# Mixture-of-experts kernel: slots of 512, 384 and 256 rows, with every slot from the ninth on inside branches

## The chip, the core and the metric

The kernel runs on one core of one Trainium2 chip. The metric is the device time of one execution in microseconds (us): the median of several runs. A profiled execution has a trace, which is read here. PE is the matrix engine (PEld its weight loads), DVE the vector engine, ACT the scalar engine, POOL GpSimd, and SP the engine that issues most DMAs. A name with a q behind it (ACTq, PEldq) is the engine's sequencer: it waits, branches, loads registers and issues DMAs.

## The reference

The reference is three layers in a row over 4608 tokens of 512 values.

```python
attn_out = _attn_ref(q, k, v)                  # linear attention, 8 x 8 heads
x = attn_out.transpose(0, 2, 1, 3).reshape(4608, 512)
# mixture of experts: 8 experts, each token goes to one
e_idx = np.argmax(x @ w_gate + modality_bias[modality_id], axis=1)
for e in range(8):
    mask = e_idx == e
    h = np.maximum(x[mask] @ w1[e], 0.0)       # 512 -> 1024
    out[mask] = gate_w[mask, None] * (h @ w2[e])   # 1024 -> 512
# a dense layer on top
h = out @ w_in                                 # 512 -> 2048
return np.maximum(0.01 * h, h) @ w_out         # 2048 -> 512
```

With the inputs used here the tokens are very unevenly spread: three experts get 1019, 2289 and 1300 tokens, the other five get none. The counts are known only on the chip, once the gate has been computed.

## The kernel before

The kernel has four stages one after another: attention with the gate (to 185 us), the experts (to 663 us), the first dense product ("hidden", to about 1045 us) and the second one. Every instruction is written out by hand in the order of each engine's queue (`manual_schedule`); an engine runs its queue strictly in that order.

**Slots.** The expert stage works on slots, groups of at most 512 tokens of one expert. `slot_tables` computes on DVE, from the counts, a small table `ti`: for each of up to 16 slots its expert, its first row in `region` (the list of token numbers) and its first column in `dense` (the output), and behind them the number of big slots and of all slots. Big slots come first. An expert with n tokens gets a big slot for each 512 tokens while more than 256 are left, and a slot of 256 rows for a rest of 1 to 256. Here that makes nine big slots (2 + 4 + 3) and one small slot.

**One slot** (`slot(s)`) is two products. `pass1` makes eight blocks of the inner layer, twelve matmuls each (L572, into PSUM bank `hp`); ACT writes relu of each as `hh` (L574), DVE the remainder `hl` (L575). The `hp` banks are three, so the fourth block has to wait until `hl` of the first has been written. `pass2` makes four blocks of the output, 24 matmuls each (L583, bank `yp`), which ACT copies out and stores to `dense` (L589, L590). One slot is thus 96 + 96 = 192 matmuls. All operands are kept as a high and a low part; `split` (L481, L482) makes the two, ACT the high one and DVE the low one.

During slot s its successor is prepared: POOL gathers the successor's tokens (`xload`, L553), ACT scales them (`xgate`), PE transposes them in the second and third block of `pass2` (`xprep`, 16 transposes, L564), SP loads the successor's weights (`wload`, L523) and ACT and DVE split them (`wsplit`).

**Static and branched slots.** The first nine slots (0 to 8) are written out without branches. In slots 0 to 7 the idle time of DVE and ACT is filled by `conversions`, which turn the 64-bit weights of the dense layers into 32-bit ones in steps; its last stores are `wod<-rh` and `wod<-rl` on SP (L635, L636). During slot 8 the first operands of the hidden stage are fetched (`pre`): SP loads the block `xr` of `dense` (L778) ahead of the slot and one of seven weight tiles `wi` (L771) at each step of it, and ACT and DVE split `xr` into operands `x` (`hidden.prep`) in the middle of the last block of `pass2`. The slots from 9 on stand in nested branches:

```python
with tc.If(ns > s):                 # ns: number of all slots
    with tc.If(nb > s) as big:      # nb: number of big slots
        slot(s)
    ...
    with big.Else():
        slot(s, rows=slice(0, SLOT // 2))
    more(s + 1)
```

Every engine executes these branches by itself, from registers that it loads from `ti` (L702, L703). Behind the branches `hidden.late` loads the rest of the first weights, `sums` and `prep` make further operands, and `hidden.run` computes (L801).

Of the kernel before, what the change touches and what calls it, by code (L numbers as in the profile page):

```python
# [421 lines left out]
CLAMP_HI = float(np.array(0x47EFFFFF, np.int32).view(np.float32))  # L422


def slot_tables(tc, con, ps, cst):


    nc = tc.nc
    V = nc.vector
    tb = con.tile([128, NE], BF16, name="ntb")  # L430
# [5 lines left out]
    d = con.tile([128, 2, 17], F32, name="sd")  # L436
    V.memset(d, 0.0)
    g = con.tile([128, 2, NE, 9], F32, name="sg")
    V.tensor_tensor(out=g[:, 0], in0=bc(n[:, :], 2, 9), in1=bc(cst["k512"], 1, NE), op=ALU.is_gt)
    V.scalar_tensor_tensor(out=g[:, 1], in0=bc(n[:, :], 2, 9), scalar=-256.0, in1=bc(cst["k512"], 1, NE), op0=ALU.add, op1=ALU.is_gt)  # L440
    m = con.tile([128, 2, NE], F32, name="sm")
    V.tensor_reduce(out=m, in_=g, axis=AX.X, op=ALU.add)
    b5 = con.tile([128, NE], F32, name="sb5")
    V.tensor_scalar(out=b5, in0=m[:, 1], scalar1=float(SLOT), scalar2=None, op0=ALU.mult)
    V.tensor_copy(out=d[:, 0, 1:9], in_=m[:, 1])
    V.tensor_tensor(out=d[:, 0, 9:17], in0=m[:, 0], in1=m[:, 1], op=ALU.subtract)
    V.tensor_tensor(out=d[:, 1, 1:9], in0=b5, in1=n, op=ALU.min)
# [5 lines left out]
    V.tensor_scalar(out=n1, in0=ci[:, 0, 16:17], scalar1=-1.0, scalar2=None, op0=ALU.add)
    sv = con.tile([128, NSLOT], F32, name="sv")
    V.tensor_scalar(out=sv, in0=cst["iota"], scalar1=n1[:, 0:1], scalar2=None, op0=ALU.min)
    ge = con.tile([128, NSLOT, 17], F32, name="ge")
    V.tensor_tensor(out=ge, in0=bc(sv[:, :], 2, 17), in1=bc(ci[:, 0], 1, NSLOT), op=ALU.is_ge)
    oh = con.tile([128, NSLOT, 16], F32, name="soh")
    V.tensor_tensor(out=oh, in0=ge[:, :, 0:16], in1=ge[:, :, 1:17], op=ALU.subtract)
    t5 = con.tile([128, 16], F32, name="t5")  # L460
    V.tensor_scalar(out=t5, in0=ci[:, 0, 0:16], scalar1=float(SLOT), scalar2=None, op0=ALU.mult)
    v = con.tile([128, 3, 16], F32, name="sv3")
    V.tensor_copy(out=v[:, 0].rearrange("p (a e) -> p a e", a=2), in_=bc(cst["e"], 1, 2))
    V.tensor_tensor(out=v[:, 1, 0:8], in0=cst["eoff"], in1=t5[:, 0:8], op=ALU.subtract)
    V.tensor_tensor(out=v[:, 1, 8:16], in0=cst["eoff"], in1=t5[:, 8:16], op=ALU.subtract)
    V.tensor_tensor(out=v[:, 1, 8:16], in0=v[:, 1, 8:16], in1=b5, op=ALU.add)
    V.tensor_tensor(out=v[:, 2], in0=ci[:, 1, 0:16], in1=t5, op=ALU.subtract)
# [17 lines left out]
def experts(ctx, tc, cst, a, region, xd, dense, did, wops, pre):  # L485
    nc = tc.nc
# [20 lines left out]
    cnt = [0, 0]  # L507
    stage, regs = {}, {}
# [25 lines left out]
    def wsplit(s, which, c):  # L534
# [7 lines left out]
        loads_to(n + 1 + AHEAD)  # L542

    def idload(s):
        if s < NSLOT:
            nc.sync.dma_start(out=idts[s % 3].rearrange("p t c -> p (t c)"),
                              in_=region[bass.ds(reg(s, 1, NE * NT), SLOT), :].rearrange("(p t) c -> p (t c)", t=4))
# [105 lines left out]
                yield  # L653
        store()

    def slot(s, step=lambda: None, mid2=lambda t: None, rows=slice(0, SLOT)):
        if s + 1 < NSLOT:
            xload(s + 1)
        for f in range(8):
            pass1(f, rows)  # L660
            if f % 2 == 0:
                wsplit(s, 2, f // 2)
            else:
                step()
        if s + 1 < NSLOT:
# [36 lines left out]
    nb = nc.values_load(ti[0:1, 3 * NSLOT:3 * NSLOT + 1], min_val=0, max_val=NSLOT)  # L702
    ns = nc.values_load(ti[0:1, 3 * NSLOT + 1:3 * NSLOT + 2], min_val=NSTATIC, max_val=NSLOT)  # L703

    def more(s):
        if s == NSLOT:
            return
        with tc.If(ns > s):  # L708
            before = dict(stage), list(cnt), nload[0]
            regs.clear()  # L710
            with tc.If(nb > s) as big:
                slot(s)
            stage.clear()
            stage.update(before[0])
            cnt[:], nload[0] = before[1:]
            regs.clear()
            with big.Else():
                slot(s, rows=slice(0, SLOT // 2))
            regs.clear()
# [271 lines left out]
def build(ctx: ExitStack, tc, a, out, dbg=None):  # L991
# [13 lines left out]
    with tc.manual_schedule():  # L1005
# [108 lines left out]
```

## Time and profile before

| | |
|---|---|
| median of 3 runs | 1421.89 us (1420.99 to 1422.07) |
| profiled execution | 1421.04 us, span of its trace 1419.2 us |
| PE busy over the span | 92% (weight loads 86%) |
| DVE, ACT, POOL busy | 74%, 41%, 20% |
| mean granted PE clock | 0.972 |
| slot 8 (static, 512 rows) on PE | 589.75 to 636.60 us |
| slot 9 (in a branch, 256 rows) on PE | 637.39 to 662.80 us |
| hidden stage starts on PE | 669.35 us |

The profile's times count from the start of the span; what lies around the span is 1421.04 - 1419.2 = 1.8 us. A busy share says how full an engine is over the whole run; what one stage is worth is read from that stage's own rows.

### The profile page before, as it was taken

To read this page: it belongs to the slowest core of one execution; us is meant where nothing else is said; L and a number is where in the kernel's file an instruction comes from. 1 tells how busy PE (TensorE), PEld (TensorE's weight loads), DVE (VectorE), ACT (ScalarE), POOL (GpSimd) and SP (SyncE) were. 2 spreads that over 40 slices of the span, in tenths; PEclk is the share of its full clock that TensorE was granted. 3 is DMA by queue.
4 is the path that set the end of the run, shared out by engine and by line. 5 is a ranking of instruction groups with operands and counts; after the bars stand their busy time and mean duration, and the time that the engine had idled before them with its cause. 6 is when DMAs were issued, how large, how long until landed. Compare 5 with 4: busy or idle time off the path is not lost.

```text
span 1419.2 us, 23583 instructions
## 1 busy us (share of the span) xinstructions
PE 1311.5 (92%) x9189; PEld 1224.6 (86%) x9189; DVE 1047.6 (74%) x1504; ACT 586.8 (41%) x924; POOL 289.0 (20%) x249
## 2 busy tenths in 40 slices
PE   5987719999999999998999999999989999999998
PEld 5876717778777877787999999999989999999998
DVE  4889846867786777746677777787767777877785
ACT  3545415455545554556223323232333333333342
POOL 0004431101110011001334343434321101111111
PEclk9999869999999999999999999999999999999999
DMA  9763246778777878686933332333595343434330
GB/s 371 284 246 127 76 156 232 259 240 279 259 255 247 275 254 263 194 311 195 407 146 134 135 119 104 136 148 120 233 417 205 122 134 123 149 120 134 119 119 30
DMA packets 146970, 279.57 MB, mean 197 GB/s; under 512 B 18208, under 2 KB 70432, under 8 KB 145952
## 3 DMA queue, kind: packets, MB, share of 16 engines
q1 hardware_dynamic: 122064, 208.46, 43.1%
q10 hardware_dynamic: 17232, 48.48, 8.7%
q0 software_dynamic: 7552, 21.02, 4.1%
q8 instruction: 75, 1.23, 0.4%
q14 instruction: 47, 0.39, 0.1%
HBM read 181.59 MB, written 96.32 MB: 196 GB/s over the span
## 4 chain that ended last, share of the span: by engine, by line
issue 26%; DVE 8%; PE 7%; POOL 6%; DMA 3%; ACT 1%; POOLq 0%; SPq 0%; DVEq 0%
PE hp L801 7%; POOL out L982 3%; DMA wi<-wid 2%; POOL s L841 2%; DVE ht L814 1%; DMA hd<-ht 1%; DVE ht L850 1%; DVE ht L847 1%; DVE s L838 1%; DVE x L482 1%; DVE ht L834 1%; DVE s L836 1%; POOL s L842 1%; DVE xl L482 0%; ACT ht L843 0%
## 5 line engine op out<-in xcount | busy, mean ns | idle before, releaser
L801 PE MATMUL hp<-xh,wi 128*128 128x256 f32 x1152 | 212.8, 281 | 4.2 <-DVE ht L850 2.3
L960 PE MATMUL yp<-wi,x 128*128 128x256 f32 x1152 | 191.2, 283 | 0.6 <-DVE x L482 0.6
L801 PEld LDWEIGHTS hp<-xh,wi 128*128 128x128 f32 x1152 | 179.4, 188 | 6.8 <-DVE ht L850 3.7
L960 PE MATMUL yp<-wi,wi 128*128 128x256 f32 x1200 | 178.2, 283 | 0.3 <-DVE wi L482 0.3
L801 PE MATMUL hp<-x,wi 128*128 128x256 f32 x1296 | 164.5, 286 | 9.2 <-ACTq L708 6.4
L801 PEld LDWEIGHTS hp<-x,wi 128*128 128x128 f32 x1296 | 161.0, 195 | 9.6 <-ACTq L708 6.6
L960 PEld LDWEIGHTS yp<-wi,wi 128*128 128x128 f32 x1200 | 163.5, 192 | 0.5 <-DVE wi L482 0.5
L960 PEld LDWEIGHTS yp<-wi,x 128*128 128x128 f32 x1152 | 161.5, 192 | 0.8 <-DVE x L482 0.8
L801 PE MATMUL hp<-xl,wi 128*128 128x256 f32 x576 | 160.7, 279 | 0.0
L553 POOL DMA_INDIRECT xg<-xd,idi x44 | 55.6, 1264 | 398.6 <-DVE hl L575 331.6
L572 PE MATMUL hp<-xh,w1h 128*128 128x512 f32 (+1 forms) x320 | 122.9, 384 | 11.8 <-DVE hl L575 11.2
L583 PE MATMUL yp<-hh,w2h 128*128 128x512 f32 (+1 forms) x320 | 122.9, 384 | 0.0
L572 PE MATMUL hp<-xl,w1h 128*128 128x512 f32 (+1 forms) x320 | 121.6, 380 | 0.0
L572 PE MATMUL hp<-xh,w1l 128*128 128x512 f32 (+1 forms) x320 | 121.6, 380 | 0.0
L583 PE MATMUL yp<-hl,w2h 128*128 128x512 f32 (+1 forms) x320 | 121.5, 380 | 0.0
L583 PE MATMUL yp<-hh,w2l 128*128 128x512 f32 (+1 forms) x320 | 121.4, 379 | 0.0
L982 POOL DMA_INDIRECT out<-yo,idx x36 | 47.4, 1317 | 315.9 <-DVE idx L976 294.3
L482 DVE TENSOR_TENSOR w1l<-st,w1h 128x1024 fp32r<-128x1024 f32 x44 | 53.8, 1227 | 76.5 <-ACT w1h L481 74.1
L801 PEld LDWEIGHTS hp<-xl,wi 128*128 128x128 f32 x576 | 108.0, 187 | 0.0
L814 DVE SCALAR_TENSOR_TENSOR ht<-ht 128x1024 f32<-128x1024 f32 x72 | 104.9, 1457 | 2.5
L841 POOL TENSOR_TENSOR s<-s,s 128x512 f32<-128x512 f32 x36 | 48.7, 1352 | 209.3 <-DVE s L838 163.8
L843 ACT ACTIVATE ht<-s 128x512 f32<-128x512 f32 x36 | 22.8, 633 | 151.5 <-POOL s L842 147.0
(202 smaller groups left out, 2583.5 us busy)
## 6 DMA issues: line engine op xcount, KB each, us to landing
st<-in_w SPq DMA_DIRECT2D x89, 512.0 KB, 6.5
hd<-ht ACTq DMA_DIRECT2D x72, 512.0 KB, 2.9
xt<-hd SPq DMA_DIRECT2D x18, 1024.0 KB, 5.3
hr<-hd SPq DMA_DIRECT2D x18, 1024.0 KB, 5.2
wi<-wid SPq DMA_DIRECT2D x28, 512.0 KB, 10.3
wi<-wod SPq DMA_DIRECT2D x6, 2048.0 KB, 13.1
v<-in_v SPq DMA_DIRECT2D x16, 650.0 KB, 9.7
k<-in_k SPq DMA_DIRECT2D x16, 576.0 KB, 9.4
```

Source lines behind the costliest of these rows:

```text
L482: nc.vector.tensor_tensor(out=lo, in0=src, in1=hi.bitcast(F32), op=ALU.subtract)
L553: nc.gpsimd.indirect_dma_start(out=xg[:, t], out_offset=None, in_=xd, in_offset=bass.IndirectOffsetOnAxis(ap=idi[:, t:t + 1], axis=0), bou ...
L572: nc.tensor.matmul(hp[:, rows], lhsT=w[:, k, 128 * f:128 * f + 128], rhs=x[:, k, rows], start=(n == 0), stop=(n == 11))
L583: nc.tensor.matmul(yp[:, rows], lhsT=w[:, f, 128 * d:128 * d + 128], rhs=h[:, f, rows], start=(n == 0), stop=(n == 23))
L801: self.nc.tensor.matmul(bank[:, g], lhsT=w[:, h, k, 128 * g:128 * g + 128], rhs=x[:, k], start=(n == 0), stop=(n == 5))
L814: V.scalar_tensor_tensor(out=c, in0=c, scalar=0.01, in1=c, op0=ALU.mult, op1=ALU.max)
L834: V.tensor_tensor(out=h[:, 0, 0], in0=bank, in1=s[1], op=ALU.add)
L836: V.tensor_tensor(out=s[6], in0=bank, in1=s[1], op=ALU.add)
L841: G.tensor_tensor(out=s[6], in0=s[6], in1=s[5], op=ALU.add)
L843: nc.scalar.activation(out=h[:, 1, 1], in_=s[5], func=AF.Relu)
L960: nc.tensor.matmul(bank, lhsT=x[:, k], rhs=w[i][:, h, k], start=(c == 0), stop=(c == 23))
L982: ins = nc.gpsimd.indirect_dma_start(out=out, out_offset=bass.IndirectOffsetOnAxis(ap=idi[s % 2][:, t:t + 1], axis=0), in_=y[:, t], in_off ...
```

## The change

The change has four parts. (1) `slot_tables` knows three sizes: a rest of 385 to 512 tokens gets 512 rows, one of 257 to 384 gets 384 rows, and one of 1 to 256 gets 256 rows. For the inputs here (1300 = 2 x 512 + 276) there are now eight big slots, one of 384 and one of 256 rows. (2) Eight slots (0 to 7) are static and all from slot 8 on stand in branches. (3) The branch on the number of slots has an Else: the last slot runs a body with `ahead=False`, which gathers, transposes, loads and splits nothing for a successor. (4) `pre` is no longer spread over a slot: all its loads and both `prep`s stand in one piece between slot 7 and the branches.

```diff
-NSTATIC = 9
+NSTATIC = 8
+SIZES = (512, 384, 256)
...
-    V.tensor_tensor(out=g[:, 0], in0=bc(n[:, :], 2, 9), in1=bc(cst["k512"], 1, NE), op=ALU.is_gt)
-    V.scalar_tensor_tensor(out=g[:, 1], in0=bc(n[:, :], 2, 9), scalar=-256.0, in1=bc(cst["k512"], 1, NE), op0=ALU.add, op1=ALU.is_gt)
+    for i in range(3):
+        V.scalar_tensor_tensor(out=g[:, i], in0=bc(n[:, :], 2, 9), scalar=float(-(384, 256, 0)[i]), in1=bc(cst["k512"], 1, NE),
+                               op0=ALU.add, op1=ALU.is_gt)
...
-    pr = con.tile([128, NSLOT, 3, 16], F32, name="spr")
+    pr = con.tile([128, NSLOT, 3, NV], F32, name="spr")
...
-    def slot(s, step=lambda: None, mid2=lambda t: None, rows=slice(0, SLOT)):
-        if s + 1 < NSLOT:
+    def slot(s, rows=slice(0, SLOT), step=lambda: None, ahead=True):
+
+        if ahead:
             xload(s + 1)
...
-        for s in range(NSTATIC - 1):
+        for s in range(NSTATIC):
             slot(s, step=lambda: next(conv, None))
         for _ in conv:
             pass
-    load, prep = pre()
-    slot(NSTATIC - 1, step=lambda: next(load, None), mid2=lambda t: prep() if t == 3 else None)
...
+    pre()
+    nb, nm, ns = (nc.values_load(...) for i in range(3))
...
+    def sized(s, ahead):
+        k = kept()
...
+        with tc.If(nb > s) as big:
+            one(0)
+        with big.Else():
+            with tc.If(nm > s) as middle:
+                one(1)
+            with middle.Else():
+                one(2)
 
     def more(s):
-        if s == NSLOT:
+        if s + 1 == NSLOT:
+            sized(s, False)
             return
...
+        k = kept()
+        with tc.If(ns > s + 1) as again:
+            sized(s, True)
             more(s + 1)
+        with again.Else():
+            restore(k)
+            sized(s, False)
...
-                    def loads():
-                        for i in ORDER:
-                            hidden.wload(0, i)
-                            yield
-
-                    return loads(), lambda: (hidden.prep(0, 1), hidden.prep(0, 2))
+                    for i in ORDER:
+                        hidden.wload(0, i)
+                    hidden.prep(0, 1)
+                    hidden.prep(0, 2)
```

Where the change moves instructions is seen in the built order of each engine. First ACT's queue before the change, from the end of slot 7 into slot 8 and, behind the dots, into slot 8's last block (`xr` is the block of `dense`, `x` its split operand, `y` the copy of an output block):

```order
L481 CAST w1h<-st_2171 128x4x256
L481 CAST rh<-r 128x1792
L574 ACTIVATE hh<-hp 128x512
L481 CAST w2h<-st_2172 128x1024
...
L481 CAST x_5256<-xr_5255 128x512 x2
L589 COPY y_2183<-yp 128x512
```

The two casts of `x` stood behind all relus of slot 8. ACT's queue at the same place after the change; the body that follows the branches here is that of 512 rows, and those of 384 and 256 rows begin alike:

```order
L486 CAST w1h<-st_2174 128x4x256
L486 CAST rh<-r 128x1792
L486 CAST x_5259<-xr_5258 128x512 x2
L710 TENSOR_LOAD ti x3
L743 COMPARE_AND_BRANCH
L730 COMPARE_AND_BRANCH
L582 ACTIVATE hh<-hp 128x512
L486 CAST w2h<-st_2175 128x1024
```

The casts now stand ahead of every relu of slot 8, and so do three register loads and the branches. The second place is PE's queue around the branched slots. Before, from the end of the static slot 8, with the body of 512 rows, its jump to the end, and the branch for the next slot behind the body of 256 rows:

```order
L583 MATMUL yp<-hl,w2h 128x512
L702 TENSOR_LOAD ti
L703 TENSOR_LOAD ti
L708 COMPARE_AND_BRANCH
L711 COMPARE_AND_BRANCH
L572 MATMUL hp<-xh,w1h 128x512
...
L711 UNCONDITIONAL_BRANCH
...
L583 MATMUL yp<-hl,w2h 128x256
L711 UNCONDITIONAL_BRANCH
L708 COMPARE_AND_BRANCH
```

After the change, from the end of the static slot 7 over the three bodies of slot 8 to the branch for the next one:

```order
L710 TENSOR_LOAD ti x3
L743 COMPARE_AND_BRANCH
L730 COMPARE_AND_BRANCH
L580 MATMUL hp<-xh,w1h 128x512
...
L730 UNCONDITIONAL_BRANCH
L733 COMPARE_AND_BRANCH
L580 MATMUL hp<-xh,w1h 128x384
...
L733 UNCONDITIONAL_BRANCH
L580 MATMUL hp<-xh,w1h 128x256
...
L743 COMPARE_AND_BRANCH
```

The body of a slot is now picked by two branches in place of one, and a body that is run stands in front of or between others that are jumped over. The third place is the end of PE's branches after the change: the last body of the Else for slot 8, which stands behind all others, and the hidden stage:

```order
L730 UNCONDITIONAL_BRANCH
L733 COMPARE_AND_BRANCH
L580 MATMUL hp<-xh,w1h 128x384
...
L733 UNCONDITIONAL_BRANCH
L580 MATMUL hp<-xh,w1h 128x256
...
L591 MATMUL yp<-hl,w2h 128x256
L733 UNCONDITIONAL_BRANCH
L829 MATMUL hp<-x_5259,wi_5260 128x256 x36
```

The Else bodies stand in the reverse order of the slots, so that slot 9's Else is followed by the three bodies of slot 8's Else, and these by the hidden stage (L829, before L801).

## Rows read from the trace of the kernel before

**Rows 1.** The page: its span, and the queue of PE's instructions (packets, MB).

```profile
span 1419.2 us, 23583 instructions
...
q8 instruction: 75, 1.23, 0.4%
```

**Rows 2.** Stages of slot 8 and 9: stretch, length, busy (instructions) by engine, clock, DMA.

```profile
589.75:636.60 46.85, 45.69 (x209) 37.42 (x207) 24.17 (x29) 24.03 (x31) 5.78 (x4) 1.00 0.80 275
637.39:662.80 25.41, 25.13 (x208) 24.82 (x208) 16.49 (x21) 18.18 (x27) 4.48 (x4) 1.00 0.67 213
```

**Rows 3.** Timeline of PE: start, length, instruction, idle time before and its releaser.

```profile
636.14 0.39 PE L583 MATMUL yp<-hh,w2l 128*128 128x512 f32 x1
636.37 0.39 PE L583 MATMUL yp<-hl,w2h 128*128 128x512 f32 x1
637.39 0.38 PE L572 MATMUL hp<-xh,w1h 128*128 128x256 f32 x1 [0.64 <-ACT y L589]
...
637.85 0.28 PE L572 MATMUL hp<-xh,w1h 128*128 128x256 f32 x1
637.97 0.28 PE L572 MATMUL hp<-xl,w1h 128*128 128x256 f32 x1
...
662.65 0.28 PE L583 MATMUL yp<-hl,w2h 128*128 128x256 f32 x1
669.35 3.33 PE L801 MATMUL hp<-x,wi 128*128 128x256 f32 x14 [6.43 <-ACTq L708]
...
703.85 4.38 PE L801 MATMUL hp<-x,wi 128*128 128x256 f32 x23 [2.78 <-DMA wi<-wid]
```

**Rows 4.** Line 711, the branch over the big body: duration ns, start us.

```profile
L711 PEldq COMPARE_BRANCH  x1: 3352/3352/3352, 634.0 to 634.0; - x1
...
L711 ACTq COMPARE_BRANCH  x1: 50/50/50, 638.8 to 638.8; - x1
```

**Rows 5.** Line 708 from 660 to 670 us, the branch out: shortest/median/longest ns, starts.

```profile
L708 PEldq COMPARE_BRANCH  x2: 192/2640/5088, 660.6 to 665.9; - x2
...
L708 ACTq COMPARE_BRANCH  x2: 37/41/45, 663.8 to 669.5; - x2
```

**Rows 6.** Line 702, the register loads ahead of the branches.

```profile
L702 PEldq TENSOR_LOAD <-ti x1: 777/777/777, 632.5 to 632.5; - x1
```

**Rows 7.** DMA queues from 634.0 to 637.5 us, the stretch of PE's first branch.

```profile
q8 instruction: 1, 0.02, 1.7%
```

**Rows 8.** Timeline of SP: start, length, DMA issued.

```profile
599.27 0.45 SPq L778 DMA_DIRECT2D xr<-dense  x1
...
670.26 0.82 SPq L771 DMA_DIRECT2D wi<-wid  x2
```

**Rows 9.** DMA issues from 598 to 600 us: size, us from issue to landing.

```profile
xr<-dense SPq DMA_DIRECT2D x1, 1024.0 KB, 7.8
```

**Rows 10.** Timeline of ACT around the start and the end of slot 8.

```profile
594.75 1.69 ACT L481 CAST rh<-r 128x1792 fp32r<-128x1792 f32 x1 [2.76 <-DVE r L631]
...
633.30 1.14 ACT L481 CAST x<-xr 128x512 fp32r<-128x512 f32 x2
```

**Rows 11.** Timeline of DVE at the start of slot 8.

```profile
598.49 0.69 DVE L575 SCALAR_TENSOR_TENSOR hl<-hp,hh 128x512 fp32r<-128x512 f32 x1
```

**Rows 12.** Waits during slot 8: us in total, times, longest.

```profile
PE hp L572 <- DVE hl L575: 1.2, 1, 1.2
```

**Rows 13.** Stretches behind the branches: length, busy by engine, clock, DMA share, GB/s.

```profile
666.00:670.00 4.00, 0.65 (x3) 0.68 (x4) 0.48 (x2) 0.00 (x0) 0.00 (x0) 0.51 0.21 72
670.00:673.00 3.00, 3.00 (x16) 3.00 (x16) 2.97 (x6) 1.87 (x4) 0.00 (x0) 0.52 0.60 160
...
676.00:700.00 24.00, 24.00 (x205) 24.00 (x204) 16.56 (x20) 5.24 (x9) 8.81 (x7) 1.00 1.03 405
```

**Rows 14.** Timeline of DVE at the end of the table.

```profile
190.53 0.95 DVE L471 TENSOR_REDUCE sr<-spr 128x48 f32<-128x768 f32 x1
```

**Rows 15.** Timeline of SP behind the table.

```profile
194.00 0.36 SPq L546 DMA_DIRECT2D idt<-region  x1
```

More of the change, by code (lines that the diff above doesn't have):

```diff
@@ L442, in slot_tables @@
+    for i in range(3):
+        V.scalar_tensor_tensor(out=g[:, i], in0=bc(n[:, :], 2, 9), scalar=float(-(384, 256, 0)[i]), in1=bc(cst["k512"], 1, NE),
+                               op0=ALU.add, op1=ALU.is_gt)
+    m = con.tile([128, 3, NE], F32, name="sm")
     V.tensor_reduce(out=m, in_=g, axis=AX.X, op=ALU.add)
     b5 = con.tile([128, NE], F32, name="sb5")
-    V.tensor_scalar(out=b5, in0=m[:, 1], scalar1=float(SLOT), scalar2=None, op0=ALU.mult)
-    V.tensor_copy(out=d[:, 0, 1:9], in_=m[:, 1])
@@ L446, in slot_tables @@
-    V.tensor_tensor(out=d[:, 0, 9:17], in0=m[:, 0], in1=m[:, 1], op=ALU.subtract)
+    V.tensor_scalar(out=b5, in0=m[:, 0], scalar1=float(SLOT), scalar2=None, op0=ALU.mult)
+    V.tensor_copy(out=d[:, 0, 1:9], in_=m[:, 0])
+    V.tensor_tensor(out=d[:, 0, 9:25].rearrange("p (a e) -> p a e", a=2), in0=m[:, 1:3], in1=m[:, 0:2], op=ALU.subtract)
     V.tensor_tensor(out=d[:, 1, 1:9], in0=b5, in1=n, op=ALU.min)
-    V.tensor_tensor(out=d[:, 1, 9:17], in0=n, in1=d[:, 1, 1:9], op=ALU.subtract)
-    ci = con.tile([128, 2, 17], F32, name="ci")
+    V.tensor_tensor(out=n, in0=n, in1=d[:, 1, 1:9], op=ALU.subtract)
@@ L450, in slot_tables @@
+    V.tensor_tensor(out=d[:, 1, 9:25].rearrange("p (a e) -> p a e", a=2), in0=d[:, 0, 9:25].rearrange("p (a e) -> p a e", a=2),
+                    in1=bc(n[:, :], 1, 2), op=ALU.mult)
+    ci = con.tile([128, 2, NV + 1], F32, name="ci")
     for f in range(2):
-        V.tensor_tensor_scan(out=ci[:, f], data0=cst["one"][:, 0:17], data1=d[:, f], initial=0.0, op0=ALU.mult, op1=ALU.add)
+        V.tensor_tensor_scan(out=ci[:, f], data0=cst["one"][:, 0:NV + 1], data1=d[:, f], initial=0.0, op0=ALU.mult, op1=ALU.add)
@@ L452, in slot_tables @@
     n1 = con.tile([128, 1], F32, name="n1")
[L453 removed]
+    V.tensor_scalar(out=n1, in0=ci[:, 0, NV:NV + 1], scalar1=-1.0, scalar2=None, op0=ALU.add)
     sv = con.tile([128, NSLOT], F32, name="sv")
     V.tensor_scalar(out=sv, in0=cst["iota"], scalar1=n1[:, 0:1], scalar2=None, op0=ALU.min)
[L456 to L457 removed]
@@ L458, in slot_tables @@
[L458 to L463, printed above, removed]
+    ge = con.tile([128, NSLOT, NV + 1], F32, name="ge")
+    V.tensor_tensor(out=ge, in0=bc(sv[:, :], 2, NV + 1), in1=bc(ci[:, 0], 1, NSLOT), op=ALU.is_ge)
@@ L464, in slot_tables @@
+    oh = con.tile([128, NSLOT, NV], F32, name="soh")
+    V.tensor_tensor(out=oh, in0=ge[:, :, 0:NV], in1=ge[:, :, 1:NV + 1], op=ALU.subtract)
+    t5 = con.tile([128, NV], F32, name="t5")
+    V.tensor_scalar(out=t5, in0=ci[:, 0, 0:NV], scalar1=float(SLOT), scalar2=None, op0=ALU.mult)
+    v = con.tile([128, 3, NV], F32, name="sv3")
+    V.tensor_copy(out=v[:, 0].rearrange("p (a e) -> p a e", a=3), in_=bc(cst["e"], 1, 3))
+    V.tensor_tensor(out=b5, in0=b5, in1=cst["eoff"], op=ALU.add)
     V.tensor_tensor(out=v[:, 1, 0:8], in0=cst["eoff"], in1=t5[:, 0:8], op=ALU.subtract)
-    V.tensor_tensor(out=v[:, 1, 8:16], in0=cst["eoff"], in1=t5[:, 8:16], op=ALU.subtract)
@@ L466, in slot_tables @@
-    V.tensor_tensor(out=v[:, 1, 8:16], in0=v[:, 1, 8:16], in1=b5, op=ALU.add)
-    V.tensor_tensor(out=v[:, 2], in0=ci[:, 1, 0:16], in1=t5, op=ALU.subtract)
-    pr = con.tile([128, NSLOT, 3, 16], F32, name="spr")
+    V.tensor_tensor(out=v[:, 1, 8:24].rearrange("p (a e) -> p a e", a=2), in0=bc(b5[:, :], 1, 2),
+                    in1=t5[:, 8:24].rearrange("p (a e) -> p a e", a=2), op=ALU.subtract)
+    V.tensor_tensor(out=v[:, 2], in0=ci[:, 1, 0:NV], in1=t5, op=ALU.subtract)
+    pr = con.tile([128, NSLOT, 3, NV], F32, name="spr")
@@ L473, in slot_tables @@
     V.tensor_tensor(out=r[:, :, 1:3], in0=r[:, :, 1:3], in1=bc(sv[:, :], 2, 2), op=ALU.add)
-    ti = con.tile([128, NSLOT * 3 + 2], I32, name="ti")
     V.tensor_copy(out=ti[:, 0:NSLOT * 3], in_=r.rearrange("p s f -> p (s f)"))
-    V.tensor_copy(out=ti[:, NSLOT * 3:NSLOT * 3 + 2], in_=ci[:, 0, 8:17:8])
-    return ti
+    V.tensor_copy(out=ti[:, NSLOT * 3:NSLOT * 3 + 3], in_=ci[:, 0, 8:25:8])
 def split(nc, hi, lo, src):
@@ L490, in experts @@
     ps2 = ctx.enter_context(tc.tile_pool(name="ps_m2", bufs=2, space=PSUM, reuse_waits="tile"))
-    ti = slot_tables(tc, ctx.enter_context(tc.tile_pool(name="tab", bufs=1, reuse_waits="tile")), ps, cst)
+    ti = wp.tile([128, NSLOT * 3 + 3], I32, name="ti")
+    with tc.tile_pool(name="tab", bufs=1, reuse_waits="tile") as tab:
+        slot_tables(tc, tab, ps, cst, ti)
     w1h = wp.tile([128, 4, F1], F32R, name="w1h")
@@ L532, in loads_to, with wsplit @@
             nload[0] += 1
-    def wsplit(s, which, c):
+    def wsplit(s, which, c, ahead=True):
         n = 8 * s + 4 * (which - 1) + c
@@ L654, in conversions @@
         store()
-    def slot(s, step=lambda: None, mid2=lambda t: None, rows=slice(0, SLOT)):
-        if s + 1 < NSLOT:
+    def slot(s, rows=slice(0, SLOT), step=lambda: None, ahead=True):
+        if ahead:
             xload(s + 1)
@@ L661, in slot @@
             if f % 2 == 0:
-                wsplit(s, 2, f // 2)
+                wsplit(s, 2, f // 2, ahead)
             else:
                 step()
-        if s + 1 < NSLOT:
+        if ahead:
             xgate(s + 1)
@@ L669, in slot @@
                           in_=idts[s % 3].rearrange("p t c -> p (t c)"))
-        idload(s + 2)
+        if ahead:
+            idload(s + 2)
         for t in range(4):
             def mid():
-                if s + 1 < NSLOT and t in (1, 2):
+                if ahead and t in (1, 2):
                     xprep(2 * t - 2)
                     xprep(2 * t - 1)
-                mid2(t)
             pass2(t, o, mid, rows)
-            if s + 1 < NSLOT:
+            if ahead:
                 wsplit(s + 1, 1, t)
@@ L699, in experts, with kept, restore, one @@
             pass
-    load, prep = pre()
-    slot(NSTATIC - 1, step=lambda: next(load, None), mid2=lambda t: prep() if t == 3 else None)
-    nb = nc.values_load(ti[0:1, 3 * NSLOT:3 * NSLOT + 1], min_val=0, max_val=NSLOT)
-    ns = nc.values_load(ti[0:1, 3 * NSLOT + 1:3 * NSLOT + 2], min_val=NSTATIC, max_val=NSLOT)
+    pre()
+    nb, nm, ns = (nc.values_load(ti[0:1, 3 * NSLOT + i:3 * NSLOT + i + 1], min_val=(0, 0, NSTATIC + 1)[i], max_val=NSLOT)
+                  for i in range(3))
+    def kept():
+        return dict(stage), list(cnt), nload[0]
+    def restore(k):
+        regs.clear()
+        stage.clear()
+        stage.update(k[0])
+        cnt[:], nload[0] = k[1:]
+    def sized(s, ahead):
+        k = kept()
+        def one(i):
+            restore(k)
+            slot(s, slice(0, SIZES[i]), ahead=ahead)
+            regs.clear()
+        with tc.If(nb > s) as big:
[5 more added lines that the diff above has]
+                one(2)
     def more(s):
-        if s == NSLOT:
+        if s + 1 == NSLOT:
+            sized(s, False)
             return
[L708 to L719, printed above, removed]
+        k = kept()
+        with tc.If(ns > s + 1) as again:
+            sized(s, True)
             more(s + 1)
+        with again.Else():
+            restore(k)
+            sized(s, False)
     more(NSTATIC)
```

10 lines of the change are left out of this document (5 added, 5 removed).

## The prediction

> **What bounds the kernel now.** I first read the page for its span, 1419.2 us [rows 1], and then the two slots that change as stretches of their own. In slot 8 PE is busy for 45.69 of 46.85 us, in slot 9 for 25.13 of 25.41, both at a granted clock of 1.00 [rows 2]. So a slot is PE's time, and columns are what it pays for. The timeline of PE gives the price of a matmul as the distance of two starts: 0.23 us with 512 columns (636.14 to 636.37) and 0.12 with 256 (637.85 to 637.97) [rows 3]. A slot has 192 of them: with 0.2267 (the stretch of slot 8 less its stall and transposes) 43.5 us at 512 columns and 23.0 at 256. No row has 384 columns; halfway gives 0.173 us, thus 33.3 us a slot, an estimate.
>
> The second thing to read is what PE does between slots, because the change moves work into branches. PE stands idle 0.64 us ahead of slot 9 and 6.43 us ahead of the hidden stage [rows 3]. The rows of the branches say why. The branch on PE's sequencer that skips one body of 512 rows takes 3352 ns from 634.0 us, while the same skip takes 50 ns on ACT [rows 4]. The jump out of everything takes PE 5088 ns from 660.6 us, and ACT comes to its next branch behind it only at 669.5, after 663.8 [rows 5]. In the stretch of the skip the queue of instructions moves one packet [rows 7], 1.23 MB over 75 packets being 16 KB each [rows 1]: so I read the 3.35 us as the wait for the instructions behind the skip. It costs little today because the sequencer runs ahead: it comes to the register loads at 632.5 [rows 6], 4.1 us before slot 8 ends at 636.6 [rows 2], and to the jump out 2.2 us before slot 9 ends at 662.8. That lead is what hides a jump. At 384 columns I take 3.1 us, between the two.
>
> [...]
>
> Behind the branches DMA is the bound, not PE: SP issues the next `wi` at 670.26 us [rows 8], 7.5 us after slot 9's end. From 676 to 700 the DMA engines are full (1.03 at 405 GB/s) [rows 13], and at 703.85 PE still has waited 2.78 us for `wi` [rows 3].
>
> **The change, part by part.**
>
> Slot 8 gets narrower: 43.5 - 33.3 = 10.2 us less. Its 16 transposes stay. The old stall in it, PE's wait of 1.2 us for `hl` [rows 12] (about 1.5 with its edges), goes into the new one: -1.5.
>
> Slot 8 gets an entry: three register loads at 0.78 us [rows 6] where there were none, and one skip over the body of 512 rows at 3.35, in all 5.7 us against a lead of 4.1. PE starts some 1.2 us late: +1.2.
>
> Slot 8 gets a new wait. ACT runs its queue in order, and the two casts of `x` now stand ahead of every relu. They need `xr`. SP issues that load only at 599.27 [rows 8], behind the last stores of the conversion, whose cast ran at 594.75 on ACT [rows 10], and it takes 7.8 us to land [rows 9]: 607.1. Nothing of the change makes its issue earlier; the slot's other loads now come behind the `wi` loads, so it meets a little less traffic, and I take 606. Then two casts in 1.14 us [rows 10], DVE's remainder of the second, a relu, and `hl` at 0.69 [rows 11]: the first bank is free at about 609.0. PE has three banks: 36 matmuls of 0.173 from 591.0 fill them by 597.2. It then stands until 609.0: +11.8 (10 to 13). Queued behind the cast on ACT are all relus and the casts of `w2`, and on DVE all `hl`; PE waits for them. At this place the entry's 1.2 us cost nothing of their own: a later start only shortens the stall.
>
> [...] Slot 8: +1.5. Sum for slot 8: -10.2 - 1.5 + 1.2 + 11.8 + 1.5 = **+2.8**.
>
> Slot 9 gets a chain of jumps, since PE's sequencer must find one body among many: out of the body of 384 rows over that of 256 (the target is near and probably fetched with what came before: 0.1 to 1.5, I take 0.9), then the far jump to the last slot's bodies (5.09; as little as 3.35), then a skip over 512 rows and one over 384 rows, 3.35 each. That is 12.7 us, less the lead of 3.1: a gap of 9.0 to 9.6, I take 9.3, where PE moved on within 0.8 (636.60 to 637.39): +8.5. Starting at the low clock costs +1.5. With no successor there are no transposes and little to stall for: 23.0 in place of 25.4, -2.4. Sum **+7.6**. That a jump is costly by waiting for instructions and not by the branch itself is what the 50 ns on ACT against 3352 on PE show [rows 4]. [...]
>
> The exit gets shorter: the last body runs out with near skips on SP, ACT, DVE and POOL, where they jumped over all 16 slots before. SP can issue `wi` some 0.4 us behind slot 9's end, not 7.46. PE has one far jump, 5.09 less a lead of 2.2, so 2.9 us idle for 6.55, and it no longer waits 2.78 us for `wi`; both and the clock give more than 7, so the DMA bound decides: **-7.0**.
>
> The tables get two more operations on DVE and wider ones: the reduction of 768 values takes 0.95 us [rows 14], with 1152 half as much again, and its product too; two small ones beside: 1.55 us in all. The next consumer, the load of `idt` at 194.00 [rows 15], follows 2.5 us behind the reduction, so some of it may be covered; I take about half: **+0.7** (0 to 1.5).
>
> The sum is 2.8 + 7.6 - 7.0 + 0.7 = **+4.1 us**. From the profiled execution, 1421.04, that makes 1425.1; the median of the runs shown is 0.85 above it, so the median becomes **1426.0**.
>
> **The rivals.**
>
> *Same as before, by cheaper jumps and an early `xr`.* If the far jump costs 3.35 like the near one (-1.7) and `xr` lands at 604 (-2), the sum is +0.4: 1422.3. For it: with two prices in one trace, 3.35 and 5.09, the far one may have been slowed by what else ran at 660 to 666. Against: right behind it, at 666 to 670, DMA moves only 72 GB/s [rows 13].
>
> *Faster: a skip over one body is free.* If PE holds the skipped instructions already, the two skips ahead of slot 9 go (-6.7), and the stop of 2.9 us left costs half as much clock (-0.8): 1426.0 - 7.5 = 1418.5. [...] For it: 3.35 was measured once, behind a whole slot of straight instructions, where the sequencer might have had little time to fetch ahead. Against: the packet in that very stretch.
>
> *Slower still: fetches and loads collide.* SP issues seven `wi` in one piece. If they hold up `xr` or the jumps (every skip at 5.09: +3.5; `xr` 2 us later: +2), the time is 1429.5 to 1431.5. For it: at the skip that I took the price from the DMA queues were nearly empty, while the new jumps come with the `wi` loads behind them. Against: seven tiles of 128 x 1024 values are 3.7 MB, at 405 GB/s [rows 13] about 9 us, long through when slot 9 begins.
>
> **How the numbers follow.** My forecast has a chance of 0.42, with a range of 1425 to 1429; the collision 0.15; the cheaper jumps 0.28; the free skip 0.15. The first two are slower, so 0.57; about 0.2% or 2.8 us is what a measurement can tell from no change, and the third falls within it (0.28), the fourth below (0.15). The range reaches from the free skip, 1418.5, to the collision, 1432; what it leaves out is a sum in which several terms miss in one direction, for example an `xr` that has landed before ACT asks (up to 11 us less).
>
> **What the new profile would show.** Right, if ACT's cast of `x` stands at about 606 with a wait of 8 us or so for the load of `xr`; if PE has one stop of 10 to 13 us within the first 36 matmuls of slot 8, released by `hl`; if PE stands some 9 us ahead of slot 9 with three branches on its sequencer of 5.1, 3.4 and 3.4 us; if the clock is 0.5 behind both stops; if SP issues `wi` within 1 us of slot 9's end. Wrong, if the skips show as 0.1 us, if `xr` is there before 600, or if the wait for `wi` stays and takes back what the exit gives.

## The result and the profile after

The changed kernel takes 1440.36 us (median of 4 runs, 1438.66 to 1441.76) where the kernel before takes 1421.44; the ratio is 1.0134, 95% interval 1.0116 to 1.0151. That is 19 us slower, against a forecast of 4, and outside the range (1418.5 to 1432). The profiled execution took 1438.66 us with a span of 1436.9, 17.6 us more than that of before, and the trace shows where they are.

PE's timeline first: start, length, instruction, idle time before and what ended it.

```profile
596.18 0.43 PE L580 MATMUL hp<-xh,w1h 128*128 128x384 f32 x1 [1.82 <-issue]
...
602.19 0.33 PE L580 MATMUL hp<-xl,w1h 128*128 128x384 f32 x1
602.37 0.34 PE L580 MATMUL hp<-xh,w1l 128*128 128x384 f32 x1
615.34 0.69 PE L580 MATMUL hp<-xh,w1h 128*128 128x384 f32 x1 [12.63 <-DVE hl L583]
615.82 0.52 PE L580 MATMUL hp<-xl,w1h 128*128 128x384 f32 x1
616.14 0.52 PE L580 MATMUL hp<-xh,w1l 128*128 128x384 f32 x1
...
646.13 0.34 PE L591 MATMUL yp<-hl,w2h 128*128 128x384 f32 x1
657.61 0.55 PE L580 MATMUL hp<-xh,w1h 128*128 128x256 f32 x1 [11.14 <-issue]
...
681.96 0.28 PE L591 MATMUL yp<-hl,w2h 128*128 128x256 f32 x1
683.70 4.57 PE L829 MATMUL hp<-x,wi 128*128 128x256 f32 x36 [1.46 <-DMA dense<-y]
...
716.49 4.55 PE L829 MATMUL hp<-x,wi 128*128 128x256 f32 x36 [2.61 <-DMA wi<-wid]
```

A matmul of 384 columns takes 0.17 us, as estimated. PE makes three blocks of slot 8 and stands for 12.63 us; then it runs at 0.32 us a matmul. It stands 11.14 us ahead of slot 9, but only 1.46 ahead of the hidden stage, where it stood 6.43 before [rows 3]. What holds slot 8 is on ACT's timeline:

```profile
599.20 1.70 ACT L486 CAST rh<-r 128x1792 fp32r<-128x1792 f32 x1 [2.76 <-DVE r L639]
611.46 1.14 ACT L486 CAST x<-xr 128x512 fp32r<-128x512 f32 x2 [10.56 <-DMA xr<-dense]
612.84 0.49 ACT L582 ACTIVATE hh<-hp 128x384 fp32r<-128x384 f32 x1 [0.24 <-issue]
```

The first relu of slot 8 comes at 612.84, behind casts that waited 10.56 us for `xr`. The branches on PE's sequencer between slot 8 and slot 9 (shortest/median/longest ns, first and last start), and the granted clock (behind the POOL column) in the 4.3 us after the first stop, during the second one, and in the 3.1 us after it:

```profile
L743 PEldq COMPARE_BRANCH  x2: 92/2611/5130, 591.9 to 643.6; - x2
L733 PEldq COMPARE_BRANCH  x2: 377/2680/4984, 643.2 to 652.5; - x2
L730 PEldq COMPARE_BRANCH  x1: 3562/3562/3562, 648.8 to 648.8; - x1
```

```profile
615.34:619.66 4.32, 4.32 (x13) 4.32 (x14) 3.14 (x4) 0.70 (x2) 3.38 (x3) 0.50 1.03 409
...
646.46:657.61 11.15, 0.01 (x2) 0.04 (x1) 1.22 (x1) 1.52 (x2) 0.00 (x0) 0.68 0.26 75
657.61:660.72 3.11, 3.11 (x14) 3.11 (x15) 0.00 (x0) 0.12 (x1) 0.00 (x0) 0.50 0.02 5
```

All this is where the prediction put it, but for the wait for `wi`, which it took as gone. One thing it did not have at all. The last matmul of the kernel ends at 1425.1 us, 10.7 later than before (1414.3), but the span ends 17.6 later. Behind the last matmul GpSimd drains its queue (the closing line of the kernel, first before and then after the change):

```profile
L1110 POOLq DRAIN  x3: 40/113/3406, 1414.8 to 1419.0; - x3
```

```profile
L1136 POOLq DRAIN  x3: 40/113/10433, 1425.6 to 1436.6; - x3
```

The longest of the three drains takes 10.4 us where it took 3.4. From stage to stage (the start of a matmul plus its spacing as the end of a slot; each row is rounded by itself) the 17.6 us are:

| stage | forecast | measured |
|---|---|---|
| up to the end of slot 7 | +0.7 | +4.5 |
| slot 8 with its entry | +2.8 | +5.3 |
| stop ahead of slot 9, and slot 9 | +7.6 | +9.6 |
| from there to the wait for `wi` (703.85, now 716.49) | -7.0 | -6.6 |
| on to the last matmul | 0 | -1.9 |
| behind the last matmul | 0 | +6.9 |

### The profile page after: what moved, and what is told of

It reads as the page before. It is cut to its first block, busy times and chain, and to the rows that moved or that the text cites. A ratio compares the mean times of both kernels' runs of the same rounds, so it can differ in the third digit from the quotient of the medians.

```text
span 1436.9 us, 23488 instructions
## 1 busy us (share of the span) xinstructions
PE 1302.1 (91%) x9173; PEld 1222.7 (85%) x9173; DVE 1039.5 (72%) x1497; ACT 575.3 (40%) x912; POOL 283.4 (20%) x245
## 4 chain that ended last, share of the span: by engine, by line
PE 31%; issue 30%; DVE 16%; POOL 7%; DMA 5%; ACT 3%; SPq 0%; DVEq 0%; POOLq 0%; ACTq 0%
PE yp L591 14%; PE hp L580 9%; PE hp L829 3%; POOL out L1010 3%; POOL s L869 3%; DVE ht L842 2%; DMA hd<-ht 2%; DVE ht L875 1%; DVE s L866 1%; DVE ht L878 1%; PE tp L572 1%; DVE ht L862 1%; PE xp L247 1%; DVE s L864 1%; DVE x L487 1%
## 5 line engine op out<-in xcount | busy, mean ns | idle before, releaser
L829 PE MATMUL hp<-xh,wi 128*128 128x256 f32 x1152 | 212.8, 281 | 4.4 <-DVE ht L878 2.4
L829 PEld LDWEIGHTS hp<-xh,wi 128*128 128x128 f32 x1152 | 179.4, 188 | 7.0 <-DVE ht L878 3.6
L829 PE MATMUL hp<-x,wi 128*128 128x256 f32 x1296 | 161.6, 283 | 4.1 <-DMA wi<-wid 2.6
L829 PEld LDWEIGHTS hp<-x,wi 128*128 128x128 f32 x1296 | 158.1, 191 | 4.4 <-DVE ht L878 2.8
L829 PE MATMUL hp<-xl,wi 128*128 128x256 f32 x576 | 160.7, 279 | 0.0
L580 PE MATMUL hp<-xh,w1h 128*128 128x512 f32 (+2 forms) x320 | 123.5, 386 | 37.1 <-DVE hl L583 24.2
L561 POOL DMA_INDIRECT xg<-xd,idi x40 | 50.6, 1265 | 377.7 <-DVE hl L583 346.1
L580 PE MATMUL hp<-xl,w1h 128*128 128x512 f32 (+2 forms) x320 | 122.0, 381 | 0.0
L580 PE MATMUL hp<-xh,w1l 128*128 128x512 f32 (+2 forms) x320 | 121.6, 380 | 0.0
L591 PE MATMUL yp<-hh,w2h 128*128 128x512 f32 (+2 forms) x320 | 120.9, 378 | 0.0
L591 PE MATMUL yp<-hl,w2h 128*128 128x512 f32 (+2 forms) x320 | 119.6, 374 | 0.0
L591 PE MATMUL yp<-hh,w2l 128*128 128x512 f32 (+2 forms) x320 | 119.5, 373 | 0.0
L829 PEld LDWEIGHTS hp<-xl,wi 128*128 128x128 f32 x576 | 108.0, 187 | 0.0
L580 PEld LDWEIGHTS hp<-xh,w1h 128*128 128x128 f32 x320 | 62.2, 194 | 51.5 <-DVE hl L583 27.9
L487 DVE TENSOR_TENSOR w1l<-st,w1h 128x1024 fp32r<-128x1024 f32 x40 | 48.8, 1224 | 67.1 <-ACT w1h L486 67.0
```

Of the source, the lines that this page charges most:

```text
L487: nc.vector.tensor_tensor(out=lo, in0=src, in1=hi.bitcast(F32), op=ALU.subtract)
L561: nc.gpsimd.indirect_dma_start(out=xg[:, t], out_offset=None, in_=xd, in_offset=bass.IndirectOffsetOnAxis(ap=idi[:, t:t + 1], axis=0), bou ...
L580: nc.tensor.matmul(hp[:, rows], lhsT=w[:, k, 128 * f:128 * f + 128], rhs=x[:, k, rows], start=(n == 0), stop=(n == 11))
L591: nc.tensor.matmul(yp[:, rows], lhsT=w[:, f, 128 * d:128 * d + 128], rhs=h[:, f, rows], start=(n == 0), stop=(n == 23))
L829: self.nc.tensor.matmul(bank[:, g], lhsT=w[:, h, k, 128 * g:128 * g + 128], rhs=x[:, k], start=(n == 0), stop=(n == 5))
```

## The experiments

The theory after the result: the casts ahead of the relus make the stop in slot 8; the skips over bodies make that ahead of slot 9; and the four gathers that the last slot no longer issues (112 gathers and scatters on GpSimd in place of 116) make the long drain. Rivals stand in the expectations. Ratios are to the kernel before, timed on the same chip, with 95% intervals.

**The splits of `xr` moved back.**

```
-    pre()
+    prep = pre()
...
-            slot(s, slice(0, SIZES[i]), ahead=ahead)
+            slot(s, slice(0, SIZES[i]), ahead=ahead, mid2=lambda t: prep() if s == NSTATIC and t == 3 else None)
...
-                    hidden.prep(0, 1)
-                    hidden.prep(0, 2)
+                    return lambda: (hidden.prep(0, 1), hidden.prep(0, 2))
```

> The changed kernel, but the two splits of xr stand in the last block of slot 8 again, inside the bodies, as before the change; its loads stay in one piece ahead of the branches. If the casts of x, which wait for the load of xr ahead of all relus, make PE stand 12.6 us in slot 8, this stop goes, and with it the 1.9 us of low clock behind it: 14.5 us less than the changed kernel, about 1426 us. Rival: the seven wi loads in one piece fill the DMA queues, so that the next thing to wait for in slot 8 (the w2 weights or the tokens of slot 9) is late instead: PE then stands as long at another place, and the time stays within 3 us of the changed kernel's 1440.

Measured: 1433.41 us, ratio 1.0081 (1.0052 to 1.0110), 7 us less than the changed kernel, between the 14.5 expected and the rival's 3. The stop of 12.6 us is gone, and about half of it comes back in other places:

```profile
604.22 0.44 PE L580 MATMUL hp<-xh,w1h 128*128 128x384 f32 x1 [2.02 <-DVE hl L583]
629.28 0.66 PE L572 MATMUL tp<-cf,xg 128*128 128x128 f32 x4 [3.06 <-DVE xl L487]
```

PE now waits 3.1 us for the transposes' banks; slot 8 takes 43.0 us from its first matmul to its last, for 50.3 in the changed kernel. Without any stop it would be some 35, an estimate from 192 matmuls at 0.173 us and the 16 transposes.

**The smallest body first.**

```
-        with tc.If(nb > s) as big:
-            one(0)
-        with big.Else():
-            with tc.If(nm > s) as middle:
+        with tc.If(nm <= s) as small:
+            one(2)
+        with small.Else():
+            with tc.If(nb <= s) as middle:
                 one(1)
             with middle.Else():
-                one(2)
+                one(0)
```

> The changed kernel with the three bodies of a slot in the reverse order, 256 rows first and 512 last, so that slot 9 falls through into its body behind the far jump, and slot 8 skips the body of 256 rows in place of that of 512. If each skip costs PE 3.6 to 5.0 us by waiting for instructions, both of slot 9 go (8.5 us), the stop ahead of slot 9 becomes 2 to 3 us for 11.1, and some of the low clock goes: 8 to 10 us less than the changed kernel, about 1431 us. Rival: the far jump alone and what is prefetched behind it set the stop, and the skips are only what is waited through: the stop stays at 7 us or more and the gain is under 4 us.

Measured: 1435.07 us, ratio 1.0085 (1.0055 to 1.0115). The branches ahead of slot 9 are now 0.38, 5.06 and 0.08 us, and PE stands 2.54 us:

```profile
649.72 0.35 PE L580 MATMUL hp<-xh,w1h 128*128 128x256 f32 x1 [2.54 <-ACT w1h L486]
```

So the two skips go with the code that was skipped: the branch into the body right behind it takes 0.08 us, where the skips took 3.56 and 4.98. The stop is 8.6 us shorter, but the medians are only 5 us apart, and 8 to 10 were expected. The trace shows where the rest goes: slot 9 and the hidden stage start 7.9 and 7.8 us sooner (hidden at 675.86 us), and the hidden stage gives 4.2 of it back. After 24 matmuls PE stops there for a cast of `x`, which the changed kernel doesn't do, and the clock is 0.52 for the 3.5 us behind it. PE's waits from 590 to 700 us (us in total, times, longest):

```profile
PE hp L829 <- ACT x L486: 2.7, 1, 2.7
```

**The last slot alone, and the tables alone.** Both are the kernel before with one part of the change.

```
-                slot(s, rows=slice(0, SLOT // 2))
+                slot(s, rows=slice(0, SLOT // 2), ahead=False)     # first kernel
```
```
-    ti = slot_tables(...)                                          # second kernel
+    slot_tables(tc, tab, ps, cst, ti)      # three sizes; nb read from the second count
```

> The kernel before with one part of the change alone: the body of 256 rows prepares no successor. Slot 9 then issues no transposes and no gathers, so there are 40 gathers on GpSimd as in the changed kernel, against 44. Slot 9 takes 23 to 24 us for 25.4 on PE; the jump out behind it stays, so 1 to 3 us less than before: about 1420 us. The end of the kernel, where GpSimd's last drain took 3.4 us before and 10.4 after the change: if the number of gathers sets it, it is 10.4 us here too, and the time is 1426 instead; if the branches do, it stays at 3.4.

> The kernel before with the tables of three sizes alone (its bodies and branches take the number of slots over 256 rows, so that it runs nine big slots and a small one as before). The tables take 1.5 us longer on DVE, of which 0.4 show in the trace of the changed kernel at the start of slot 0. If the 3 us that slot 0 is longer after the change (its wait for the first conversion load is 3.4 us for 1.9, and the clock falls behind it) come of the tables, slot 0 takes 51.8 us here too and the time is 1424 to 1426; if they are chance or come of the rest of the change, slot 0 takes 48.9 and the time is 1421 to 1422.

Measured: the last slot alone takes 1425.97 us, ratio 1.0018 (1.0002 to 1.0034); its last matmul ends at 1407.6 in the trace, 6.8 us sooner than before, and its drain takes 10.4 us and gives all of that back. The branches stand as before, so the new branches don't make the drain long. The 6.8 us are more than the 1 to 3 expected: slot 9 gives 2.3 (23.1 us for 25.4), and the stretch from its end to the wait for `wi` gives 4.2 (36.9 us for 41.1), since PE stands only 1.94 us ahead of the hidden stage and SP issues `wi` 3.65 us behind slot 9's end, not 7.46.

The tables alone take 1422.94 us, ratio 1.0001 (0.9985 to 1.0018): what they cost is within some 2.5 us of nothing. Slot 0 took 51.5 us in their trace, not 48.9. It took 51.2 to 53.4 us in all nine traces with the new tables, but also 52.0 and 52.2 in two of the five with the old ones (48.8 to 49.6 in the other three). So a long slot 0 doesn't need the new tables; whether they make it more frequent stays open.

**Does the number of gathers decide?** Three kernels: the changed one with the gathers of slot 3 issued twice (116 again), the kernel before with the same (120), and the kernel before whose last slot prepares nothing but still gathers (116). The first edit is that of the first two kernels, the second that of the third against the last slot alone.

```
             xload(s + 1)
+            if s == 3:
+                xload(s + 1)
```
```
-        if ahead and s + 1 < NSLOT:
+        if s + 1 < NSLOT:
             xload(s + 1)
```

> The changed kernel with the four gathers of slot 3 issued twice, so that GpSimd issues 116 gathers and scatters in the execution, as before the change, and not 112; the branches are as changed. If their number sets how long GpSimd's last drain takes (3.4 us with 116, 10.4 with 112 in five of five traces so far), the drain is 3.4 us again and the time 6.9 us less than the changed kernel, about 1433.5. Rival: the drain is longer because the last slot's path through the branches leaves something open on GpSimd; then it stays 10.4 us and the time stays at 1440.

> The kernel before with the four gathers of slot 3 issued twice: 120 of GpSimd's DMAs. A count below some number making the drain long would leave 3.4 us here and the time at 1421 to 1422; a drain that depends on where the count stands when the kernel ends would show another value than 3.4 or 10.4. The stop of 1.5 us ahead of the 114th DMA of before tells where the count stands: it should come four DMAs earlier in the output stage.

> The kernel before, with a body of 256 rows that prepares no successor but for the gathers, which it still issues (116 of GpSimd's DMAs in all). In the run without these gathers PE ended 6.8 us sooner than before and the drain gave it all back. If the number decides, PE ends 6.8 us sooner again and the drain stays 3.4 us: about 1414.5 us, faster than the kernel before. Rival: as for the first run of this call, the drain is 10.4 us and the time that of before, 1421.

Measured: with 116 the changed kernel's drain is 3.42 us, with 120 that of before is 3.59. Both times miss the expectation, 1450.12 and 1437.56 us (ratios 1.0191 and 1.0097), because the doubled gathers hold up slot 3, which takes 62.6 and 61.5 us for 46.8. In the first of these traces the second cast of the gathers' indices (`idi`) waits 14.1 us on DVE for the first gathers to land, and every `hl` of slot 3 stands behind it; 1440.4 - 6.9 + 15.8 is 1449. The last kernel is faster than before: 1416.53 us, ratio 0.9967 (0.9953 to 0.9981), with a drain of 3.42 us. The last slot alone, first without its gathers and then with them:

```profile
L1112 POOLq DRAIN  x3: 40/113/10432, 1408.1 to 1419.1; - x3
```

```profile
L1112 POOLq DRAIN  x3: 40/113/3419, 1408.3 to 1412.5; - x3
```

The stop ahead of the 114th gather or scatter (2.47 us idle, for 1.00 at the second scatter of the next pairs) came four DMAs earlier in the output stage with 120, as expected.

**How many are needed?** The changed kernel with one gather in the last slot, and with two.

```
-        if ahead:
-            xload(s + 1)
+        if s + 1 < NSLOT:
+            xload(s + 1, 4 if ahead else 1)      # 2 in the other kernel
```

> The changed kernel with one gather in the last slot: 113 of GpSimd's DMAs. The stop ahead of the 114th has been seen in every trace with 116 or 120, at the same number, and the drain was long in every trace with 112. If the long drain is the work that otherwise comes ahead of the 114th, 113 leave it at the end: 10.4 us of drain and about 1440 us. Rival: the drain depends on the number in another way (a multiple of four, or the last slot's gathers at all), and is 3.4 us: 1433.5.

> The changed kernel with two gathers in the last slot: 114 of GpSimd's DMAs, so that the last of all is the 114th. If that number decides, the stop of 1.5 us comes ahead of the very last scatter, the drain is 3.4 us, and the time is 5 to 7 us less than the changed kernel, about 1434. Rival: it needs 116, and the drain is 10.4 us as in the changed kernel: 1440.

Measured: 1440.49 us with 113, 1434.57 with 114 (ratios 1.0136 and 1.0091). The drains with 113 and with 114, GpSimd's last DMAs with 114, and for comparison the last of the 112 in the changed kernel and the 114th of 116 in the kernel before:

```profile
L1136 POOLq DRAIN  x3: 40/113/10515, 1423.4 to 1434.5; - x3
```

```profile
L1136 POOLq DRAIN  x3: 40/113/3321, 1427.7 to 1432.0; - x3
```

```profile
1423.73 0.97 POOL L1010 DMA_INDIRECT out<-yo,idx  x1 [16.39 <-DVE idx L1004]
1427.96 0.98 POOL L1010 DMA_INDIRECT out<-yo,idx  x1 [3.26 <-issue]
```

```profile
1425.80 0.97 POOL L1010 DMA_INDIRECT out<-yo,idx  x1 [1.78 <-DVE yo L1006]
```

```profile
1396.42 0.98 POOL L982 DMA_INDIRECT out<-yo,idx  x1 [2.48 <-issue]
```

The 114th starts 1.5 us later than a last scatter does elsewhere (3.26 us idle, for 1.78), waiting for nothing that the profile shows, and the drain is short. GpSimd's queue also holds some `INC_SWDGE_SEM` instructions, whose number differs between these kernels; but the late start comes at the 114th gather or scatter with two of them in front of it (the kernel before) as with four (the kernel with 114), so in these two it goes by the number of gathers and scatters.

**The loads of `xr` and `wi` and the splits alone**, in the kernel before: all in one piece ahead of its static slot 8.

```
-    slot(NSTATIC - 1, step=lambda: next(load, None), mid2=lambda t: prep() if t == 3 else None)
+    for _ in load: pass
+    prep()
+    slot(NSTATIC - 1)
```

> The kernel before with one part of the change alone: the loads of xr and wi and the splits of xr stand in one piece ahead of slot 8, which stays static and 512 rows wide. If the casts of x hold all relus of slot 8 until xr has landed, PE fills three banks in 8.2 us and then stands for 10 to 13 us, with 1.9 us of low clock behind: 12 to 15 us more than before, 1435. Rival: at 512 rows there is more cover and the seven loads in one piece are what holds slot 8 of the changed kernel: the stop is under 6 us and the time under 1430.

Measured: 1435.65 us, ratio 1.0085 (1.0058 to 1.0112). The stop is there at 512 rows too, and this part by itself makes the kernel 14 us slower by the medians, 12 by the ratio:

```profile
602.86 0.39 PE L572 MATMUL hp<-xh,w1l 128*128 128x512 f32 x1
614.87 0.79 PE L572 MATMUL hp<-xh,w1h 128*128 128x512 f32 x1 [11.62 <-DVE hl L575]
```

**All together.** Smallest body first and gathers kept in the last slot; one kernel has the `wi` loads spread over slot 8 and the splits in its last block, the other has the loads of `xr` and `wi` and the splits in the last slot. Of each edit one line is shown.

```
+            load = loads() if s == NSTATIC else iter(())      # first kernel
+            load = iter(()) if ahead else loads()             # second kernel
```

> The changed kernel with all that the runs so far point to: the splits of xr in the last block of slot 8, the seven wi loads one at each step of slot 8, bodies with the smallest first, and gathers in the last slot (116 in all). Against the run with the smallest body first (1435): the stop of 13.3 us and its 1.9 us of low clock go, the drain gives 6.9 us back, some 2 us of small stops in slot 8 come: about 1415 us. Rival: as with the splits alone moved, PE waits in slot 8 for the transposes or the weights, 5 us and low clock: 1420 or more.

> Three sizes with everything the runs have pointed to: the smallest body first, gathers in the last slot (116 of GpSimd's DMAs), and the loads of xr and of the seven wi tiles and the splits of xr in the body of the last slot, where nothing is loaded for a successor (there the DMA engines were busy for 0.16 of the time). Slot 8 then has the DMA queues to itself. If the wi loads in slot 8 are what made the far jump 6.2 us in place of 5.1 and the jump ahead of it 2.5 in place of 0.4, the stop ahead of slot 9 falls from 5.8 to about 2.5 us, and slot 8 and 9 lose some 3 us of small stops: about 1413 us, less than both kernels and than the kernel before with only its last slot changed (1416.5). Rival: the jumps are as long because of the place of the bodies; the stop stays at 5 to 6 us and the time at 1418.

Measured: 1418.63 us, ratio 0.9975 (0.9962 to 0.9987), and 1416.22 us, ratio 0.9958 (0.9942 to 0.9973): both slightly faster than the kernel before (0.25 and 0.42%), and neither as fast as expected (1415 and 1413). The branches out of slot 8, with the loads in slot 8 and with the loads in the last slot:

```profile
L735 PEldq COMPARE_BRANCH  x1: 2468/2468/2468, 632.9 to 632.9; - x1
...
L745 PEldq COMPARE_BRANCH  x1: 6183/6183/6183, 635.4 to 635.4; - x1
```

```profile
L735 PEldq COMPARE_BRANCH  x1: 377/377/377, 631.6 to 631.6; - x1
...
L745 PEldq COMPARE_BRANCH  x1: 5317/5317/5317, 632.0 to 632.0; - x1
```

In the first the DMA share was 1.02 from 620 to 636 us, in the second 0.53 from 628 to 637.6; the stop ahead of slot 9 is 5.75 and 2.80 us. In this pair the jumps among full queues are dearer: 2.47 us for 0.38 and 6.18 for 5.32. The second kernel misses its 1413, since the hidden stage gives back what it gains by starting sooner: from its first matmul to the end of the wait for `wi` it takes 37.1 us (662.21 to 699.29), for 32.8 in the changed kernel. It is no faster than the kernel before with only its last slot changed (1416.53), timed apart from it: what the narrower slot 8 gains and what the branches cost come out about even.

## Why the prediction was wrong

**The end of the kernel** is the step that failed. The sum took what lies behind the last matmul as unchanged, and took the last slot's dropped gathers, by leaving them out of it, as free. They cost 6.9 us in the trace. The runs agree: 113 against 114 gathers and scatters in the changed kernel is 5.9 us (the 114th starts 1.5 late there), and the last slot alone without and with its gathers is 0.5% or some 7 us by the ratios, 6.6 in the traces. Without this term the median would be about 1433.5, still 1.5 above the range and 7.5 above the forecast. What is left are terms that were too small: the chain by 2.0 us, the stop in slot 8 with its entry by 2.5 and the stretch ahead of it by 3.8, less 1.5 gained behind slot 9.

**The stop in slot 8** was right in mechanism and place, and nearly in size: 12.6 us for 11.8, released by `hl`, behind casts that wait for `xr`; moving the casts removed it and the piece alone makes it. `xr` landed at 611.4 and not at 606, because slot 7 ended 4.5 us later; its 7.7 us are those of before [rows 9]. The entry took 2.0 us for 1.2, since its skip took 3.97 us and not 3.35. The 1.5 us for a start at the low clock, which the sum has in both slots, were an estimate from the start of the hidden stage before [rows 3, 13]; such a start took 1.9 us in slot 8 (13 matmuls at 0.32 for 0.17, clock 0.50) and 1.4 in slot 9 (14 matmuls in 3.11 us for some 0.12 each, clock 0.50).

**The chain ahead of slot 9** was right in mechanism and too small: 11.1 us for 9.3. The near jump was cheaper (0.38 for 0.9), the far one as taken (5.13), the first skip 3.56, but the second, right behind the first, 4.98 and not 3.35. The free skip, the rival for a faster kernel, is refuted: two skips cost 8.5 us, and without them (smallest body first) the stop was 2.54 us for 11.14. In the 11.15 us of the stop the queue of instructions (q8) moved three packets, 0.05 MB, which fits the reading that PE's sequencer waits for instructions there.

**The exit** was right in size: -6.6 us to the same wait for `wi` for the -7.0 forecast, and SP issues `wi` at 682.27, as slot 9 ends. Its working was right only in part. The wait for `wi`, which the prediction took as gone, is still there (2.61 us for 2.78), and the near skips are not the whole cause: the last slot alone, whose branches still lead over all 16 slots, already has 4.2 of the 6.6 us. The 1.9 us more come behind that wait: the next 36 matmuls take 4.55 us, where before the first 23 took 4.38 [rows 3] and the clock was 0.83 over 700 to 710.

**Up to slot 8** the forecast was 0.7, and the trace has 4.5: 1.4 us are there ahead of the tables, in work that the change doesn't touch, 0.3 are the tables, and 2.95 are slot 0, where a wait for the first conversion load grew from 1.9 to 3.4 us and the clock fell to 0.62 for the 4.5 us behind it. Executions of the kernel before alone spread from 1419.2 to 1428.2 us (19 runs), so this may be chance of the profiled pair. Against that, slot 0 is long in every trace with the new tables; the cause stays open.

**The rivals.** The slower one, collision of fetches and loads, came nearest and was still 9 us short (1429.5 to 1431.5), and for another reason: jumps under full queues do get dearer (6.2 for 5.1 us), but in the changed kernel the queues were nearly empty there (0.26). The cheaper jumps with an early `xr` are refuted by the far jump's 5.13 us and the 7.7 us of `xr`.

## What to carry to other kernels

Work that is dropped because nobody needs it can have been paying for something (here 6.9 us of drain): look at the end of the kernel, behind the last matmul, and at every queue whose count of transfers changes. ACT's relus waited here behind a cast in front of them that itself waited 10.56 us, so work for a later stage belongs behind the work of this one. Where an engine branches over unrolled bodies, put the body that is wanted next straight behind the jump (its branch took 0.08 us here, and two skips 8.5), and keep the DMA queues empty there (the far jump took 5.32 us here at a DMA share of 0.53, and 6.18 at 1.02).

## What the runs showed of the hardware

GpSimd's last drain took 10.4 to 10.5 us with 112 or 113 indirect DMAs (gathers and scatters) on GpSimd (10.43 in the changed kernel and with the last slot alone, 10.52 with 113) and 3.3 to 3.6 with 114, 116 or 120 (3.32 with 114; 3.41 in the kernel before, 3.42 with 116 in the changed kernel and in the last slot with its gathers; 3.59 with 120). The start of the 114th came 1.5 us late: 2.48 us idle in the kernel before and 2.47 with 120, for 1.00 at the second scatter of neighbouring pairs, and 3.26 with 114, for 1.78 at a last scatter. What is done there is not seen in the profile, and stays open. Of the two skips in a row on PE in the changed kernel the second took 4.98 us, the first 3.56. The length of a stop alone didn't tell whether PE's granted clock fell behind it: behind stops of 2.70 us (smallest body first, hidden stage) and 2.78 us (the kernel before) it fell, to 0.52 over 3.5 us and 0.74 over 6.2 us, and behind stops of 2.61 us (the changed kernel) and 2.80 us (loads in the last slot, ahead of slot 9) it stayed at 1.00.
